# Output-projection products inside the attention's tail, a bank for the w1 sums, and w1 turns behind an exponential

## The chip, the cores and the metric

The kernel runs on one NeuronCore of a Trainium2 chip. The metric is the device time of one execution in microseconds (us); lower is better. A NeuronCore has TensorE (PE; its weight loads are shown as PEld), VectorE (DVE), ScalarE (ACT), GpSimd (POOL) and SyncE (SP), each with its own instruction queue that is worked in order, and 16 DMA engines. Here SP issues all loads. Accumulators lie in PSUM banks of 128 partitions by 512 floats.

## The reference

Two layers, each a single-token attention over a cache of 16384 positions and an MLP, both with residuals. The same weights and caches serve both layers. The kernel returns the output and the gradients of nine inputs.

```python
B, Sq, D = 2, 1, 1024
Hq, Hkv, Sk, Dh = 32, 4, 16384, 128      # F = 3584

def _A_ref(x, k_cache, v_cache, wq, wo):
    q = (x @ wq) -> [B, Hq, Sq, Dh]
    k, v = k_cache, v_cache repeated 8 times over heads
    p = softmax(einsum("bhqd,bhkd->bhqk", q, k) * Dh ** -0.5)
    return einsum("bhqk,bhkd->bhqd", p, v) reshaped to [B, Sq, Hq * Dh] @ wo

def _B_ref(x, w1, b1, w2, b2):
    return gelu(layernorm(x) @ w1 + b1) @ w2 + b2

x = x + _A_ref(layernorm(x), ...);  x = x + _B_ref(layernorm(x), ...)
x = x + _A_ref(layernorm(x), ...);  x = x + _B_ref(layernorm(x), ...)
# reference: this output, and its vjp for A_x, the caches, wq, wo, w1, b1, w2, b2
```

## The kernel before, in words

The program issues instructions in the order in which it is written; nothing reorders them between engines but semaphores. It runs the forward of layer 0, the forward of layer 1, the backward of layer 1, then the backward of layer 0 with the outputs.

*Loads.* Weights and cache tiles are 1 MB each and share one pool, `ld`, of `NLD` = 7 buffers. `w_take` (L353) takes the next buffer in turn and issues the load on SP's queue. A load waits there until the buffer's earlier contents have been read for the last time, and the loads behind it wait with it.

*A matrix times two columns.* `w_fwd` (L366) clears a part of the bank `ACCT` (called `acc_all` in the profile), then takes the tiles of a matrix one by one; `fwd_rows` (L358, its matmuls at L362) issues 32 matmuls for each, the weight tile as stationary operand, summing into the bank. wo has eight tiles, each of four heads of both batch rows; w1 has seven.

*Attention forward.* `attn_fwd` (L612) goes over eight groups `g` (batch row b = g // 4, key head g % 4), each of 16 slots. In a slot a piece of K is transposed (`emit_T`, L531), copied, and multiplied with the queries (`score`, L684). When a group's scores are complete, `post` plans its rest into later slots: maximum, 16 exponentials (`ex`, L648), 8 quads of 8 matmuls taken from a queue (`quad`, L563), each summing V times the exponentials into one half of `ACCT`: even groups the first half, odd groups the second. Then `evac` copies the sum out, `reduce` (L578) adds its parts, and `finish` (L661) scales the result into `oT`. The loop goes on after the 128 slots until the queue is empty: this is the tail, in which the groups 6 and 7 are finished. Afterwards two copies (L868) bring `oT` into `o_all`, the layout that wo's matmuls read, and wo is multiplied with `w_fwd`.

*MLP of layer 1.* `ln2_fwd` (L230) normalizes; w1 is multiplied through `w_fwd` with `keep`, an object `Back` that keeps the seven w1 tiles in their buffers for the backward and turns (transposes) them there: tiles 0 to 3 on VectorE (L294), tiles 4 to 6 on TensorE with copies by ScalarE (L395, L159). Two quarters of the tiles 4 and 5 are turned between the forward's tiles; what is left of 4 and 5 and one quarter of 6 come after the last one, ahead of the bias, the gelu (`g_u`, exponential at L894) and its slope. `weights_down` then multiplies the kept w1 tiles with the MLP's gradient `dh_all` (spread by `spg` and `Gw`, sums in the banks `dm_d` and `dm_p`, cleared in `banks`, L444 and L447), which frees their buffers for the backward's eight wo tiles; the backward attention follows.

PSUM banks of the kind `px` are handed out in turn, four of them.

Of the kernel before, what the change touches and what calls it, by code (L numbers as in the profile page):

```python
# [10 lines left out]
F32 = mybir.dt.float32  # L11
I32 = mybir.dt.int32
ACT = mybir.ActivationFunctionType
ALU = mybir.AluOpType
# [9 lines left out]
def kernel(  # L24
# [25 lines left out]
    V = nc.vector  # L50
# [3 lines left out]
    B, _, D = A_x.shape  # L54
    _, HKV, SK, DH = A_k_cache.shape
# [41 lines left out]
    def px(shape, dtype, name):  # L97
        return ps_x.tile(shape, dtype, name=name, tag="x")
# [46 lines left out]
    def copies_on(e):  # L145
        only["e"] = e
        load["A"] = load["D"] = 0.0
# [215 lines left out]
                          rhs=x[:, j0 + j, :].unsqueeze(1).to_broadcast([128, nw // 2, 2]),  # L363
                          start=False, stop=True, skip_group_check=True)

    def w_fwd(W, n_in, n_out, x, between=None, keep=None):  # L366
        JO = n_out // 128
        nw = min(WIDE, 512 // JO)
        fps = ACCT[:, 0:JO * nw].rearrange("p (j b) -> p j b", b=nw)
        V.memset(fps, 0.0)  # L370
        if keep is not None:
            keep.fps, keep.x, keep.nw = fps, x, nw
            for k in range(len(keep.tiles)):
                keep.load(k)
            last = len(keep.tiles) - 1
            for k in range(len(keep.tiles)):
                keep.forward(k)
                if keep.by_tile[k]:
                    keep.some(k)
                elif k < last:  # L380
                    keep.some(k, 2)
            return fps[:, :, 0:2]
        for j0, nj, c0, cw in w_tiles(W, n_in, n_out):
            fwd_rows(fps, nw, w_take(W, j0, nj, c0, cw), x, j0, c0 // 128)
            if between:
                between.popleft()()
        while between:
            between.popleft()()
        return fps[:, :, 0:2]
# [219 lines left out]
                sc_.later(2, a.reduce)  # L609
            sc_.q.append(fin)  # L610

    def attn_fwd(l, q_bf, rbc, oT, groups):  # L612
        sch = Sched()
        slots = [(g, c, b) for g in groups for c in range(NCH) for b in range(NB)]
        kTs, sc, st = {}, {}, {}

        def max_half(g, f):
            m = small.tile([128, 8], F32, name="mx%d" % f)
            V.tensor_reduce(out=m[:], in_=sc[g][f][:], axis=AX.X, op=ALU.max)
            charge("D", 0.7)  # L620
            st[g].append(m)

        def post(g):
            max_half(g, 1)
            m0, m1 = st[g]
            V.tensor_tensor(out=m0[:], in0=m0[:], in1=m1[:], op=ALU.max)
            esum = small.tile([128, 2, 8], F32, name="esum")
            negm = small.tile([128, 8], F32, name="negm")
            box = {}

            def p1():
                box["pm"] = pm_([8, 128], F32, "pm")
                PE.transpose(box["pm"][:, :], m0[:], identf[:])
                gm = small.tile([8, 1], F32, name="gm")
                V.reduce_max(out=gm[:], in_=box["pm"][:, :], axis=AX.X)
                box["dg"] = small.tile([8, 8], F32, name="dg")
                V.tensor_scalar(out=box["dg"][:], in0=identf[0:8, 0:8], scalar1=gm[:, 0:1], scalar2=None, op0=ALU.mult)
                charge("D", 0.5)

            def p2():  # L640
                pm2 = pm_([128, 8], F32, "pm2")
                PE.matmul(pm2[:], lhsT=onesf[0:8, :], rhs=box["dg"][:], start=True, stop=True)
                V.tensor_scalar(out=negm[:], in0=pm2[:], scalar1=-1.0, scalar2=None, op0=ALU.mult)  # L643
                charge("D", 0.2)

            def ex(f, h):
                half = NP // 2
                S.activation(out=e_all[:, g, f * half:(f + 1) * half, l, h, :],  # L648
                             in_=sc[g][f][:, h, :].rearrange("p (a b) -> p a b", b=2),
                             func=ACT.Exp, bias=negm[:, h:h + 1], scale=1.0, accum_out=esum[:, f, h:h + 1])  # L650
                charge("A", 0.3)

            def fin1():
                V.tensor_tensor(out=esum[:, 0, :], in0=esum[:, 0, :], in1=esum[:, 1, :], op=ALU.add)

            def fin2():
                pm3 = part_sum(esum[:, 0, :], 8, "pm3")
                V.reciprocal(out=rbc[:, g, :], in_=pm3[:])

            def finish(ps):  # L660
                V.tensor_tensor(out=oT[:, g, :], in0=ps, in1=rbc[:, g, :], op=ALU.mult)  # L661

            a = Acc(g, "V", lambda u: e_all[:, g, u, l].rearrange("p h t -> p (h t)"), finish, g % 2)
            sch.later(2, p1)
            sch.later(4, p2)
            for i in range(16):
                sch.later(5 + i // 2, lambda i=i: ex(i // 8, i % 8))
            sch.later(9, lambda: queue_acc(sch, a, range(0, 2), False))
            sch.later(13, lambda: queue_acc(sch, a, range(2, 4), True))
            sch.later(14, fin1)  # L670
            sch.later(15, fin2)

        def score(s):
            g, c, b = slots[s]
            if c == 0 and b == 0:
                sc[g] = {}
                st[g] = []
            kT = kTs.pop(s)
            for j in range(8):
                t = c * TC + b * 8 + j  # L680
                f = t // TH
                if t % TH == 0:
                    sc[g][f] = px([128, 8, TH], F32, "sc")
                PE.matmul(sc[g][f][:, :, t % TH], lhsT=kT[:, j, :], rhs=q_bf[:, g, :], start=True, stop=True)  # L684
            if c == NCH // 2 - 1 and b == NB - 1:
                max_half(g, 0)
            if c == NCH - 1 and b == NB - 1:
                post(g)

        cv = None  # L690
        s = 0
        while s < len(slots) + 2 or sch.busy():
            sch.s = s
            if s < len(slots):
                g, c, b = slots[s]
                if b == 0:
                    cv = kv_load("K", g, c)
                kTs[s] = emit_T(cv, b, True)
            sch.run_slot(1 if s < len(slots) else 2)
            if 2 <= s < len(slots) + 2:  # L700
                score(s - 2)
            s += 1

    def attn_bwd(l, do_bf, dqT, dn, groups, ahead):
# [148 lines left out]
    def lsl(l):  # L853
        return slice(2 * l, 2 * l + 2)

    def attn_layer_fwd(l, xT, between=None):
        y, rstd = ln_fwd(xT[:], f"a{l}")
        V.tensor_copy(out=n_all[:, 0:DJ, lsl(l)], in_=y[:])
        qps = w_fwd(A_wq, D, HD, n_all[:, 0:DJ, lsl(l)], between)
        qT_bf = vec.tile([128, G, 8], BF16, name=f"qT_bf{l}")  # L860
        for b in range(2):
            V.tensor_scalar(out=qT_bf[:, b * HKV:(b + 1) * HKV, :].rearrange("p k r -> p (k r)"), in0=qps[:, :, b],
                            scalar1=QSCALE, scalar2=None, op0=ALU.mult)
        rbc = vec.tile([128, G, 8], F32, name=f"rbc{l}")
        oT = vec.tile([128, G, 8], F32, name=f"oT{l}")
        attn_fwd(l, qT_bf, rbc, oT, ALLG)
        for b in range(2):
            V.tensor_copy(out=o_all[:, 0:HQ, 2 * l + b], in_=oT[:, b * HKV:(b + 1) * HKV, :].rearrange("p k r -> p (k r)"))  # L868
        aps = w_fwd(A_wo, HD, D, o_all[:, 0:HQ, lsl(l)])
        xn = vec.tile([128, DJ, 2], F32, name=f"xA{l}")  # L870
        V.tensor_tensor(out=xn[:], in0=aps, in1=xT[:], op=ALU.add)
        saved[f"a{l}"] = dict(y=y, rstd=rstd, qT_bf=qT_bf, rbc=rbc, oT=oT)
        return xn

    def mlp_hidden(l, xT, keep=None):
        y2, rstd2 = ln2_fwd(xT[:], f"m{l}")
        V.tensor_copy(out=m_all[:, 0:DJ, lsl(l)], in_=y2[:])
        if keep is not None:
            copies_on("A")
        hps = w_fwd(B_w1, D, F, m_all[:, 0:DJ, lsl(l)], keep=keep)  # L880
        if keep is not None:
            for k in range(len(keep.tiles)):
                keep.some(k, 1 if k == len(keep.tiles) - 1 else 4)
            copies_on(None)
        hpre = vec.tile([128, FJ, 2], F32, name=f"hpre{l}")
        V.tensor_tensor(out=hpre[:], in0=hps, in1=b1T[:].to_broadcast([128, FJ, 2]), op=ALU.add)
        x2 = wrk.tile([128, FJ, 2], F32, name="g_x2")
# [5 lines left out]
        z = wrk.tile([128, FJ, 2], F32, name="g_z")  # L893
        S.activation(out=z[:], in_=u[:], func=ACT.Exp, scale=2.0 * GELU_C)  # L894
        if keep is not None:
            V.tensor_scalar(out=x2[:], in0=x2[:], scalar1=3.0 * GELU_A * GELU_C * 0.5, scalar2=GELU_C * 0.5,
                            op0=ALU.mult, op1=ALU.add)
            V.tensor_tensor(out=x2[:], in0=x2[:], in1=hpre[:], op=ALU.mult)
# [55 lines left out]
    def weights_down(l, gT, name, mid=None):  # L954
        sv = saved[f"m{l}"]
        w1b = sv.pop("w1", None)
        if w1b is None:
            w1b = w1_back()
            for k in range(len(w1b.tiles)):
                w1b.load(k)  # L960
        w1b.banks()
        w1b.open(dh_all[:, 0:FJ, lsl(l)])
        copies_on("A")
        if l == 1:
# [738 lines left out]
```

## Time and profile before

| | |
|---|---|
| times of three runs | 1116.38, 1118.36, 1119.42 us; median 1118.36 |
| the profiled execution | 1124.0 us, of which 1122.2 us from the first to the last instruction (span) |
| busy: PE, PEld, DVE, ACT, POOL | 919.0, 674.1, 615.2, 532.3, 69.0 us |
| DMA | 441.83 MB, mean 394 GB/s over the span |
| granted TensorE clock, mean | 0.852 of full |
| forward attention of layer 1, its last result | at 419.06 us |
| w1 forward of layer 1, first and last matmul | 432.79 to 446.7 us |
| first product with a kept w1 tile | at 453.79 us |

Busy time is time in which an engine had an instruction in work. The chain of work that ended last is followed back from the last instruction, at each step to what released it. A line of the timeline gives start, duration, engine, source line, operation, output and inputs, and in brackets the idle time before it with what ended it. For DMA issues, start and duration are those of the issue on SP's queue, not of the transfer. All times are counted from the start of the span.

### The profile page before, as it was taken

The numbers are of one execution on the slowest core, as the hardware profiler recorded it, in microseconds if no ns is written. First come the engines' busy times: TensorE is split into PE (matmuls) and PEld (weight loads), VectorE is DVE, ScalarE is ACT, GpSimd is POOL, SyncE is SP. The second block draws the span as 40 slices with busy tenths as digits, with TensorE's granted clock in tenths as the row PEclk, the third lists the DMA queues.
The fourth block names the chain that finished last, engine by engine and source line by source line (L and its number), as shares of the span: only waits on it lengthen the run. The fifth ranks groups of instructions, "written<-read, shape, count | busy, mean of one in ns | idle before, by whom it ended". The sixth has DMA issues, their size and how long they took to land.

```text
span 1122.2 us, 37948 instructions
## 1 busy us (share of the span) xinstructions
PE 919.0 (82%) x16706; PEld 674.1 (60%) x16707; DVE 615.2 (55%) x1333; ACT 532.3 (47%) x1352; POOL 69.0 (6%) x122
## 2 busy tenths in 40 slices
PE   3979796458889886789987877889898896999996
PEld 3867674357677656678765676655554453455552
DVE  1545442071355434554443357479698775787776
ACT  0535352004545341334433234468587775686765
POOL 0000000000000000000000000022021111111210
PEclk9989786557899876899988899999799897797878
DMA  9999999999999988799999999998999999999997
GB/s 370 423 424 425 423 425 415 395 413 420 423 413 424 423 311 302 287 426 420 387 415 422 392 398 327 376 355 312 405 367 420 424 418 424 405 400 420 422 408 290
DMA packets 99973, 441.83 MB, mean 394 GB/s; under 512 B 7126, under 2 KB 10198, under 8 KB 62688
## 3 DMA queue, kind: packets, MB, share of 16 engines
q1 hardware_dynamic: 82464, 347.12, 76.7%
q0 software_dynamic: 17344, 92.29, 20.0%
q8 instruction: 130, 2.13, 0.7%
q14 instruction: 35, 0.29, 0.1%
HBM read 340.80 MB, written 98.58 MB: 392 GB/s over the span
## 4 chain that ended last, share of the span: by engine, by line
PE 50%; DMA 31%; DVE 11%; ACT 4%; issue 4%; POOL 0%; DVEq 0%; SPq 0%; POOLq 0%; ACTq 0%
DMA kv_V<-in_A_v_cache_dram 10%; PE tp L531 10%; DMA wt<-in_B_w_dram 5%; PE tpm L1610 5%; DMA kv_K<-in_A_k_cache_dram 5%; PE acc_all L563 4%; PE xm L1419 4%; DMA wt<-in_A_wo_dram 4%; PE xm L1333 3%; PE sc L684 3%; PE dp L1472 3%; PE wtp L395 2%; DMA keepK<-in_A_v_cache_dram 2%; PE dp L779 2%; DMA out_dram<-keepK 2%
## 5 line engine op out<-in xcount | busy, mean ns | idle before, releaser
L159 ACT COPY kT<-tp 128x512 int32<-128x512 int32 x201 | 118.0, 587 | 289.3 <-PE tp L531 277.0
L162 DVE COPY kT<-tp 128x1024 bf16<-128x1024 bf16 x167 | 114.2, 691 | 136.5 <-PE tp L531 126.3
L531 PE MATMUL tp<-ident,kv_K 128*128 128x128 bf16 x1728 | 145.3, 233 | 4.0 <-DMA kv_K<-in_A_k_cache_dram 3.7
L531 PEld LDWEIGHTS <-kv_K 128*128 128x128 bf16 x1728 | 110.2, 104 | 4.8 <-DMA kv_K<-in_A_k_cache_dram 4.5
L170 DVE CAST big<-xm 128x512 bf16<-128x512 f32 x133 | 86.4, 685 | 23.7 <-PE xm L1419 13.4
L167 ACT CAST big<-xm 128x512 bf16<-128x512 f32 x151 | 82.1, 595 | 24.9 <-PE xm L1333 13.4
L684 PEld LDWEIGHTS <-kT 128*128 128x128 bf16 x2048 | 76.3, 98 | 27.6 <-issue 22.1
L684 PE MATMUL sc<-qT_bf,kT 128*128 128x8 bf16 x2048 | 91.8, 171 | 0.0
L167 ACT CAST keepV<-xm 128x512 bf16<-128x512 f32 (+1 forms) x137 | 75.1, 594 | 32.2 <-PE xm L1419 20.3
L362 PEld LDWEIGHTS <-wt 128*128 128x128 bf16 x1920 | 57.2, 104 | 54.6 <-DMA wt<-in_B_w_dram 16.6
L159 ACT COPY wt<-wtp 128x512 int32<-128x512 int32 x70 | 39.0, 587 | 89.9 <-PE wtp L395 79.4
L648 ACT ACTIVATE e_all<-sc,negm 128x64 bf16<-128x64 f32 x256 | 77.2, 342 | 1.1 <-DVE negm L643 1.0
L170 DVE CAST keepV<-xm 128x512 bf16<-128x512 f32 (+1 forms) x101 | 66.0, 685 | 21.1 <-PE xm L1419 14.2
L531 PE MATMUL tp<-ident,kv_V 128*128 128x128 bf16 x864 | 70.1, 228 | 5.8 <-DMA kv_V<-in_A_v_cache_dram 4.4
L563 PE MATMUL acc_all<-kv_V,e_all 128*16 128x256 bf16 x864 | 46.6, 296 | 28.9 <-DMA kv_V<-in_A_v_cache_dram 13.8
L294 DVE STREAM_TRANSPOSE wt<-wt 128x512 int32<-128x512 int32 x106 | 64.5, 674 | 7.7 <-PE w2b_f L362 5.6
L531 PEld LDWEIGHTS <-kv_V 128*128 128x128 bf16 x864 | 55.5, 102 | 7.6 <-DMA kv_V<-in_A_v_cache_dram 4.7
L648 ACT ACTIVATION_READ_ACCUMULATOR e_all<-sc,negm 128x1 f32 x256 | 59.4, 232 | 0.0
L167 ACT CAST keepK<-xm 128x512 bf16<-128x512 f32 x98 | 52.8, 595 | 11.5 <-PE xm L1419 7.5
L1472 PE MATMUL dp<-wdo,kT 128*128 128x64 bf16 x896 | 52.7, 206 | 0.0
L1419 PE MATMUL xm<-QmK,blk 64*128 64x512 bf16 x256 | 47.7, 437 | 2.3 <-ACT keepV L167 1.0
L170 DVE CAST keepK<-xm 128x512 bf16<-128x512 f32 x69 | 44.8, 684 | 8.6 <-PE xm L1419 6.6
(380 smaller groups left out, 1557.7 us busy)
## 6 DMA issues: line engine op xcount, KB each, us to landing
kv_K<-in_A_k_cache_dram SPq DMA_DIRECT2D x81, 1024.0 KB, 12.5
kv_V<-in_A_v_cache_dram SPq DMA_DIRECT2D x81, 1024.0 KB, 12.0
wt<-in_B_w_dram SPq DMA_DIRECT2D x35, 1024.0 KB, 12.9
wt<-in_A_wo_dram SPq DMA_DIRECT2D x32, 1024.0 KB, 8.7
out_dram<-big POOLq DMA_DIRECT2D x26, 1024.0 KB, 17.1
out_dram<-keepV POOLq DMA_DIRECT2D x19, 1024.0 KB, 17.5
out_dram<-keepK POOLq DMA_DIRECT2D x17, 1024.0 KB, 16.2
wt<-in_A_wq_dram SPq DMA_DIRECT2D x16, 1024.0 KB, 10.9
```

Of the source, the lines that this page charges most:

```text
L159: S.copy(out=dst.bitcast(I32), in_=src.bitcast(I32))
L162: V.tensor_copy(out=dst, in_=src)
L167: S.copy(out=dst, in_=src)
L170: V.tensor_copy(out=dst, in_=src)
L294: V.transpose(out=w, in_=w)
L362: PE.matmul(fps[:, o0 + o, :].rearrange("p (a b) -> p a b", b=2), lhsT=wv[:, j, o * 128:(o + 1) * 128], rhs=x[:, j0 + j, :].unsqueeze(1).t ...
L531: PE.transpose(tp[:, j, :], cv[:, b * 8 + j, :], ident[:])
L563: PE.matmul(self.acc[cg:cg + 16, :], lhsT=coef(u), rhs=self.cv[:, t:t + 2, :].rearrange("p t d -> p (t d)"), start=False, stop=True, tile_ ...
L648: S.activation(out=e_all[:, g, f * half:(f + 1) * half, l, h, :], in_=sc[g][f][:, h, :].rearrange("p (a b) -> p a b", b=2), func=ACT.Exp, ...
L684: PE.matmul(sc[g][f][:, :, t % TH], lhsT=kT[:, j, :], rhs=q_bf[:, g, :], start=True, stop=True)
L1419: PE.matmul(pss[k][:], lhsT=blk[p:p + 64, o + 2 * h + k // 2, :], rhs=Qm[p:p + 64, :, :].rearrange("p a b -> p (a b)"), start=True, stop=T ...
L1472: PE.matmul(dp[:, :, t:t + 4], lhsT=kT[:, j, :], rhs=wd[:, :, x:x + 4], start=(b + j == 0), stop=False)
```

## The change

The change concerns four places of the forward.

1. `finish` writes each group's result twice, first into `o_all`, then into `oT`; the two copies after the attention go.
2. `attn_fwd` calls `tail(step)` after each slot beyond the 128th, where the step counts from 0. In layer 1, at step 6, `tail` clears the first half of `ACCT`, issues the first seven loads of wo, multiplies tile 0, issues the load of tile 7 and multiplies tile 1; at the steps 7 to 10 it multiplies the tiles 2 to 5. Tiles 0 to 5 hold the heads of the groups 0 to 2 and 4 to 6; tiles 6 and 7 need groups 3 and 7 and follow the attention. In layer 0 all eight tiles follow the attention as before. In TensorE's order, tiles 0 to 4 now stand ahead of the first quad of group 7, tile 5 behind it, then the other 40 matmuls of the first part, the row sums and the last 16. The order of SP's loads stays as it was.
3. At step 9 a `px` bank `h_ps` is taken and cleared, and layer 1's w1 sums go there and not into `ACCT`; the clearing between the layernorm and w1 goes. The clearing of `dm_d` and `dm_p` moves from behind `dh_all` into the layernorm, behind its first row sum.
4. The rest of TensorE's w1 turns is issued behind the exponential of the gelu: in ScalarE's order the exponential stands ahead of five copies that it stood behind. TensorE's own order is the same there.

```diff
-    def w_fwd(W, n_in, n_out, x, between=None, keep=None):
+    def w_fwd(W, n_in, n_out, x, between=None, keep=None, bank=None):
         JO = n_out // 128
         nw = min(WIDE, 512 // JO)
-        fps = ACCT[:, 0:JO * nw].rearrange("p (j b) -> p j b", b=nw)
-        V.memset(fps, 0.0)
+        fps = (ACCT if bank is None else bank)[:, 0:JO * nw].rearrange("p (j b) -> p j b", b=nw)
+        if bank is None:
+            V.memset(fps, 0.0)
...
-    def attn_fwd(l, q_bf, rbc, oT, groups):
+    def attn_fwd(l, q_bf, rbc, oT, groups, tail=lambda step: None):
...
             def finish(ps):
+                kv = g % HKV
+                V.tensor_tensor(out=o_all[:, kv * 8:(kv + 1) * 8, 2 * l + g // HKV], in0=ps, in1=rbc[:, g, :], op=ALU.mult)
                 V.tensor_tensor(out=oT[:, g, :], in0=ps, in1=rbc[:, g, :], op=ALU.mult)
...
+            if s >= len(slots):
+                tail(s - len(slots))
             s += 1
...
-        attn_fwd(l, qT_bf, rbc, oT, ALLG)
-        for b in range(2):
-            V.tensor_copy(out=o_all[:, 0:HQ, 2 * l + b], in_=oT[:, b * HKV:(b + 1) * HKV, :].rearrange("p k r -> p (k r)"))
-        aps = w_fwd(A_wo, HD, D, o_all[:, 0:HQ, lsl(l)])
+        tiles = w_tiles(A_wo, HD, D)
+        fps = ACCT[:, 0:DJ * WIDE].rearrange("p (j b) -> p j b", b=WIDE)
+        wvs = {}
+
+        def take(k):
+            wvs[k] = w_take(A_wo, *tiles[k])
+
+        def prod(k):
+            fwd_rows(fps, WIDE, wvs.pop(k), o_all[:, 0:HQ, lsl(l)], tiles[k][0], 0)
+
+        def tail(step):
+            if l == 0:
+                return
+            if step == 6:
+                assert 0 not in Acc.in_use
+                V.memset(fps, 0.0)
+                for k in range(NLD):
+                    take(k)
+                prod(0)
+                take(NLD)
+            if 6 <= step < 11:
+                prod(step - 5)
+            if step == 9:
+                h_bank[l] = px([128, 512], F32, "h_ps")
+                V.memset(h_bank[l][:, 0:FJ * (512 // FJ)], 0.0)
+
+        attn_fwd(l, qT_bf, rbc, oT, ALLG, tail)
+        if l == 0:
+            V.memset(fps, 0.0)
+            for k in range(len(tiles)):
+                take(k)
+                prod(k)
+        else:
+            for k in list(wvs):
+                prod(k)
+        aps = fps[:, :, 0:2]
...
     def mlp_hidden(l, xT, keep=None):
-        y2, rstd2 = ln2_fwd(xT[:], f"m{l}")
+        y2, rstd2 = ln2_fwd(xT[:], f"m{l}", keep.banks if keep is not None else lambda: None)
...
-        hps = w_fwd(B_w1, D, F, m_all[:, 0:DJ, lsl(l)], keep=keep)
-        if keep is not None:
-            for k in range(len(keep.tiles)):
-                keep.some(k, 1 if k == len(keep.tiles) - 1 else 4)
-            copies_on(None)
+        hps = w_fwd(B_w1, D, F, m_all[:, 0:DJ, lsl(l)], keep=keep, bank=h_bank.get(l))
...
         S.activation(out=z[:], in_=u[:], func=ACT.Exp, scale=2.0 * GELU_C)
         if keep is not None:
+            for k in range(len(keep.tiles)):
+                keep.some(k, 1 if k == len(keep.tiles) - 1 else 4)
+            copies_on(None)
             V.tensor_scalar(out=x2[:], in0=x2[:], scalar1=3.0 * GELU_A * GELU_C * 0.5, scalar2=GELU_C * 0.5,
                             op0=ALU.mult, op1=ALU.add)
...
             w1b = w1_back()
             for k in range(len(w1b.tiles)):
                 w1b.load(k)
-        w1b.banks()
+            w1b.banks()
         w1b.open(dh_all[:, 0:FJ, lsl(l)])
```

More of the change, by code (lines that the diff above doesn't have):

```diff
@@ L854, in lsl @@
         return slice(2 * l, 2 * l + 2)
+    h_bank = {}
     def attn_layer_fwd(l, xT, between=None):
```

## The prediction

> **What bounds the kernel now.** I read the page first: over the span the DMA engines are near full (394 GB/s) and TensorE is busy 82%, so the useful place to look is where DMA is *not* full. The chain of work that ended last, between 410 and 460 us (start, length, what):
>
> ```profile
> 410.05 4.86 ACT e_all L648 x32
> ...
> 419.85 6.18 PE acc_all L362 x224
> ...
> 426.39 14.06 DMA wt<-in_B_w_dram
> 440.50 1.02 PE acc_all L362 x32
> ...
> 449.77 0.59 ACT wt L159
> 450.35 0.16 ACT g_z L894
> ```
>
> Seven wo tiles are multiplied only after the attention has ended (224 matmuls from 419.85), then the chain waits for w1 tiles, then the gelu's exponential sits behind ScalarE's copies of turned w1 tiles. Next, busy time by stretches of 4 us (span, PE, PEld, DVE, ACT, POOL, PEclk, DMA share, GB/s):
>
> ```profile
> 412.00:416.00 4.00, 2.94 (x49) 1.47 (x49) 0.17 (x1) 2.90 (x20) 0.00 (x0) 0.50 0.98 377
> 416.00:420.00 4.00, 2.65 (x28) 1.92 (x29) 1.31 (x6) 0.00 (x0) 0.00 (x0) 0.50 0.10 37
> 420.00:424.00 4.00, 4.00 (x156) 4.00 (x154) 0.00 (x0) 0.00 (x0) 0.00 (x0) 0.50 0.44 108
> 424.00:428.00 4.00, 2.74 (x104) 2.64 (x101) 0.00 (x0) 0.00 (x0) 0.00 (x0) 0.81 1.04 401
> ...
> 444.00:448.00 4.00, 3.77 (x70) 3.47 (x68) 1.12 (x6) 1.97 (x4) 0.00 (x0) 0.75 0.08 26
> 448.00:452.00 4.00, 1.54 (x24) 1.33 (x22) 1.37 (x7) 2.09 (x5) 0.00 (x0) 1.00 0.00 0
> 452.00:456.00 4.00, 2.26 (x96) 2.07 (x95) 1.82 (x9) 0.00 (x0) 0.00 (x0) 0.60 0.02 4
> ```
>
> DMA stands still twice: about 6 us (0.90x4 + 0.56x4 = 5.8) around 420, and 12.5 us from 444.3 to 456.8. Why the first: the waits of SP's queue, and the instruction that its wait holds (us in total, times, longest; then start, duration):
>
> ```profile
> SPq L356 <- PE acc_all L362: 17.4, 6, 11.3
> ```
>
> ```profile
> 409.18 0.37 SPq L356 DMA_DIRECT2D wt<-in_A_wo_dram  x1
> 420.89 0.37 SPq L356 DMA_DIRECT2D wt<-in_A_wo_dram  x1
> ```
>
> Tile 6 of wo is issued at 409.18, tile 7 only at 420.89: all seven load buffers are full of wo tiles, and the first is freed when its 32 matmuls are done. The eighth tile of wo and seven of w1 stand behind that one wait.
>
> **The change, part by part, against the profiled span of 1122.2 us.** *The loads of wo tile 7 and w1.* Group 6's result is written at 410.80 (`oT`, 0.17). In the new order the result row, the copy to `oT`, and the memset of the sums (0.27) follow on a VectorE that is idle until 414.93; TensorE starts wo tile 0 at about 411.5. A tile is 32 matmuls at 27.6 ns (6.18 us / 224) = 0.88 us. SP's order is unchanged, so tile 7 is issued near 412.4, w1 tiles 0 to 3 near 413.3 to 416, and tile 4 after wo tile 5 near 417.4. Tile 6's load takes 8.8 us from issue to landing (median of that one issue), so it lands at 418.0. A landing follows the last by 2.6 us in a fed queue (w1 matmuls that wait for DMA start at 435.32, 437.94, 440.50), so tile 7 lands at 420.6; before, its matmuls started at 427.27. Shift 6.7 us. The w1 tile that decides is the fifth: before, it started 13.23 us after wo tile 7 (440.50), and from there TensorE runs without a gap (two rounds of 16 turns at 1.72 between three tiles) to 446.7. Bounds of the shift at that tile: 7.2 if every tile takes 2.55 us after 418.0; 5.7 if the handover is as in layer 0, where the queue was never empty and the fifth w1 tile came 14.24 us after wo's last (205.79 to 220.03). I take **6.7**, the spacing of this very stage.
>
> *Does anything else become last?* TensorE: tiles 0 to 4 (4.4 us) end at 415.9, quads of group 7 8x64 ns, tile 5 0.88, 40 quads at 59 ns (1.88/32) 2.4, row sums and 16 quads 1.5 (415.95 to 417.5 before), evacuation 0.44, `o_ps` 1.02, result 0.17: attention ends at 422.8, 3.4 us later than before (419.4). But only 64 matmuls remain (1.8 us), so `xA` comes at 424.7 instead of 428.27. Layernorm to `m_all` takes 3.9 us (428.27 to 432.16); the two `dm` memsets (0.27 each) fill the 0.49 us wait for its row sum; the memset of 504 columns (0.48) moves from behind `m_all` to VectorE's idle time near 412, into a bank of its own. w1 starts at 428.7, tiles 0 to 3 (four of 1.02) end at 432.8, the fifth lands at 433.8: one us of slack. VectorE turns w1 tiles 0 to 3 (16 in 9.61 us), from 429.1 to 438.7; `hpre` is due at 440.0: 1.3 us of slack. So 3.6 us of earlier `xA` are hidden by the stream; without it they would be the gain. wo tiles 4 and 5 must be in place at 415.0 and 416.4; counting back from 418.0 by 2.6 they land at 412.8 and 415.4. Group 7's 48 quads stand behind them on TensorE.
>
> *The exponential.* `g_u` ends at 447.69, the exponential ran at 450.25, behind five copies of 0.53 to 0.59. In front of them it runs at 447.72, and its result is used at 448.0 instead of 450.53: 2.5 us. What it displaces: the last three rounds of TensorE's turns need banks that those copies free. From the first copy (now 448.0) to the end of the fifth round it took 2.52 us (447.21 to 449.73), so TensorE is free at 450.5, and `dh_all` is ready at 450.3: nearly level. `spg` 0.29, then `Gw` 0.40 without two memsets ahead of it (it began at 453.33, after 452.87 + 0.54): first `dm_d` product at 451.3 against 453.79, 2.5 us. That is with the granted clock of 1.00 of the row at 448. At 0.50 eight turns take 0.87 instead of 0.46 (the forward's `tp` pieces), the fifth round ends 0.7 us later: 1.75. Gain 1.75 to 2.5, I take **2.2**, since the shifted stage begins near an edge of a clock stretch.
>
> On that clock the Trainium skill ("TensorE: Matmul & The Clock Gate", Part 4: PE-mode transpose) says that transposes do not count as busy for the clock gate. The row at 448, granted 1.00 after 4 us made up mostly of turns, doesn't bear that out; by the rule the term would be 1.75.
>
> *Small parts.* Eight more result writes of 0.17 in each layer lie under VectorE's idle time; in layer 0 the two copies (0.32) and the wait for them go, but its loads run without a pause (DMA share 1.01 to 1.05 from 160 to 245), so nothing is gained; without that cover it would be 0.2.
>
> *Behind it.* The first `dm_d` product frees the first buffer for the backward's wo loads (issued 454.86 before), and from 456.8 to 640 DMA share is 1.00: a fed stream, whose end moves with its start. Sum 6.7 + 2.2 = **8.9**: span 1122.2 to 1113.3. The profiled execution took 1124.0; the median of three is 1118.36 (1116.38 to 1119.42), so 1118.4 - 8.9 = **1109.5**.
>
> A rule speaks against the first term: the Trainium skill ("DMA: Bandwidth & Descriptors", Specifications) puts HBM at about 358 GB/s a core. The rows of this stage show 401, and 377 where it ran out. By the rule a tile of 1.05 MB takes 2.9 us, and eight behind 418.0 would gain some 2.3 us less.
>
> **Rivals.** *A: as summed*, own range 7.5 to 9.7 (5.7 + 1.75, 7.2 + 2.5) and a us or so of spread either way: 1107 to 1112.
>
> *B: another wait takes the place.* VectorE's turns or TensorE's order become last. If w1 starts 2 us later than reckoned, its turns end at 440.7 and `hpre` loses 0.7; if the turns behind the exponential also hold `spg` for all of what it saved, 2.2 go. For it: slacks of only 1.0 and 1.3 us. Against: both are computed at the lower clock, and 3.4 us stretches of steady matmuls should raise it (the row at 424 shows 0.81 after the busy one at 420). 1118.4 - 6.0 = 1112.4.
>
> *C: it doesn't do what it says.* Tile 7's load is not issued earlier, or its gain is hidden. Were SP held until the attention's end, the first term is gone and the second stays under the spread: 1116. For it: SP's queue is one line, and everything waits behind one release. Against: the release is tile 0's last matmul, in the new order ahead of group 7's quads.
>
> *D: slower.* The backward and the stores, 490 to 1122, run at granted clocks of 0.92, 0.91 and 0.87, and stretches of it move with the phase of the work. Price: 0.41 us per eight turns at half clock. To eat 8.9 and lose another 3.4, 30 groups of eight must fall to half clock, some 40 us of the 632 at a group per 1.3 us. For it: TensorE holds half of the chain. Against: the three runs before, whose phases differ too, lie within 3.0 us. About 1122.
>
> **How the numbers follow.** A 0.68, B 0.14, C 0.11, D 0.07. About 0.3% (3.4 us, 1115.0) can be told from no change. A and B are faster (0.82, and 0.03 of C and D), C is mostly no change, D mostly slower: 0.85, 0.09, 0.06. The time is A's, 1109.5. For 8 in 10 the range takes A and B whole and a part of C: 1105.5 to 1114.5; its lower end leaves room for TensorE at full clock in the attention's tail, which A's sum doesn't count.
>
> **What would show it.** Right: tile 7 of wo issued near 412.4; no row with a DMA share under 0.9 between 412 and 436; `xA` near 424; the fifth w1 tile's matmuls near 433.8; the exponential within 0.1 us of `g_u`; the first `dm_d` product near 444.9; the backward's first wo issue 8.9 us earlier. Wrong: a pause of DMA near 420 that remains, w1 matmuls that no longer wait for DMA, a TensorE wait for ScalarE just before `spg` over 1 us, or the 8.9 us there at 480 and not at the end.

## The result, and the profile after

| | before | changed | ratio, 95% interval |
|---|---|---|---|
| first comparison, 4 runs each | 1118.89 us (1116.38 to 1119.85) | 1108.88 us (1107.22 to 1109.43) | 0.9904 [0.9875, 0.9933] |
| second comparison, 17 and 6 runs | 1118.20 us (1113.78 to 1123.47) | 1108.37 us (1103.49 to 1110.11) | 0.9908 [0.9886, 0.9929] |

The change takes off 10.0 us in the first comparison and 9.8 in the second. The profiled execution of the changed kernel took 1108.78 us with a span of 1107.0. The one of before had 1122.2, which is 15.2 more; that difference must not be read as the change, as is shown below.

The chain of waits after (start, length, what), for the stretch whose chain of before stands in the prediction:

```profile
410.44 3.98 PE acc_all L362 x143
414.42 1.90 issue
416.32 0.64 PE acc_all L362 x17
...
424.03 1.86 PE acc_all L362 x64
...
430.26 3.56 PE h_ps L362 x128
433.83 1.02 PE h_ps L362 x32
...
437.09 0.31 issue
...
441.14 0.23 DVE g_u L927
441.39 0.25 ACT g_z L929
441.64 0.48 ACT wt L159
```

Of the 224 wo matmuls that stood in one piece behind the attention, 64 are left (424.03). The link of 14.06 us in which the chain waited for w1's transfers is gone: 160 w1 matmuls follow each other from 430.26, and from 408 to 446 us the chain has no DMA link at all, in both profiles of the changed kernel. What ends last in this stretch is now TensorE's order through the attention's tail, no longer the stream of loads. The exponential stands directly behind `g_u`, and the first copy behind it. New are long links called "issue", of which this stretch of the chain before had none over 0.05 us: 1.90 us in which TensorE waited for nothing that the profile names, in the middle of a wo tile, and 0.31 us among the w1 tiles.

Busy time by stretches of 4 us after (span, PE, PEld, DVE, ACT, POOL, PEclk, DMA share, GB/s):

```profile
412.00:416.00 4.00, 2.42 (x91) 2.31 (x87) 0.17 (x1) 1.91 (x14) 0.00 (x0) 0.50 1.05 405
416.00:420.00 4.00, 3.68 (x89) 2.69 (x93) 0.00 (x0) 0.00 (x0) 0.00 (x0) 0.50 1.06 411
420.00:424.00 4.00, 3.21 (x38) 2.01 (x27) 0.85 (x4) 0.00 (x0) 0.00 (x0) 0.50 1.04 401
...
432.00:436.00 4.00, 4.00 (x114) 3.90 (x111) 4.00 (x7) 0.25 (x1) 0.00 (x0) 0.50 0.99 368
436.00:440.00 4.00, 3.69 (x77) 3.54 (x75) 4.00 (x8) 1.88 (x4) 0.00 (x0) 0.57 0.38 131
440.00:444.00 4.00, 2.93 (x55) 2.58 (x53) 3.43 (x16) 2.49 (x6) 0.00 (x0) 1.00 0.00 0
444.00:448.00 4.00, 2.48 (x157) 2.14 (x157) 0.97 (x3) 0.58 (x1) 0.00 (x0) 1.00 0.27 88
448.00:452.00 4.00, 3.57 (x104) 3.38 (x103) 0.45 (x1) 1.66 (x3) 0.00 (x0) 1.00 0.99 326
```

The pause of DMA around 420 (share 0.10 and 0.44 before) is filled: 1.04 to 1.06. The second pause remains and lies earlier, from about 438 to 447. Read down the DMA column: what the change removes is idle transfer time, and the second hole, 9 us of it, is what is left in this region. The cause of the first pause, on SP's queue, is gone too (start, duration of the issues):

```profile
411.49 0.37 SPq L356 DMA_DIRECT2D wt<-in_A_wo_dram  x1
412.35 8.93 SPq L356 DMA_DIRECT2D wt<-in_B_w_dram  x5
```

wo tile 7 is issued 1.6 us after group 6's result (409.91), and the w1 loads follow at once.

How far the gain travels (times from the start of each span; the kernel before and the changed one were each profiled twice):

| event | before | before, 2nd | changed | changed, 2nd |
|---|---|---|---|---|
| wo tile 6 lands | 417.95 | 418.25 | 418.22 | 417.79 |
| wo tile 7 lands | 427.22 | 427.89 | 420.78 | 420.35 |
| fifth w1 tile lands | 440.45 | 440.84 | 433.78 | 433.32 |
| layer 1's attention sums `xA` | 428.27 | 428.94 | 425.91 | 426.04 |
| hidden sums `hpre` | 446.74 | 447.13 | 440.41 | 440.57 |
| first `dm_d` product | 453.79 | 454.17 | 444.82 | 444.98 |
| first wo load of the backward | 454.86 | 455.24 | 445.50 | 445.65 |
| backward attention begins | 488.37 | 490.81 | 479.30 | 479.88 |
| its layer-0 sums begin (`xM`) | 669.82 | 670.30 | 660.46 | 660.80 |
| from there to the end | 452.4 | 443.7 | 446.5 | 445.8 |

Up to the `xM` row, pair against pair, the change is worth 9.4 to 9.5 us (at single marks on the way 9.0 to 10.9); the medians of the runs say 9.8 to 10.0. The last row is a stretch with the same code in all four, and it varies by 8.7 us between two executions of the same kernel. So the ends of two traces can't be compared for a change of this size; a stage in front of that stretch can.

### The profile page after: what moved, and what is told of

Same layout as the page of the kernel before. It is cut to its first block, busy times and chain, and to the rows that moved or that the text cites. A ratio compares the mean times of both kernels' runs of the same rounds, so it can differ in the third digit from the quotient of the medians.

```text
span 1107.0 us, 37959 instructions
## 1 busy us (share of the span) xinstructions
PE 904.7 (82%) x16706; PEld 667.4 (60%) x16707; DVE 615.9 (56%) x1345; ACT 531.0 (48%) x1352; POOL 68.7 (6%) x122
## 4 chain that ended last, share of the span: by engine, by line
PE 51%; DMA 29%; DVE 12%; issue 4%; ACT 3%; POOL 0%; SPq 0%; DVEq 0%; ACTq 0%; POOLq 0%
PE tp L532 11%; DMA kv_V<-in_A_v_cache_dram 9%; PE acc_all L564 5%; PE tpm L1648 5%; DMA kv_K<-in_A_k_cache_dram 5%; DMA wt<-in_B_w_dram 4%; PE xm L1457 4%; DMA wt<-in_A_wo_dram 4%; PE sc L687 3%; PE xm L1371 3%; PE dp L1510 3%; PE wtp L396 2%; DMA keepK<-in_A_v_cache_dram 2%; PE dp L784 2%; DMA out_dram<-keepK 2%
## 5 line engine op out<-in xcount | busy, mean ns | idle before, releaser
L687 PEld LDWEIGHTS <-kT 128*128 128x128 bf16 x2048 | 76.3, 98 | 27.6 <-issue 22.1
L564 PE MATMUL acc_all<-kv_V,e_all 128*16 128x256 bf16 x864 | 46.4, 295 | 27.6 <-DMA kv_V<-in_A_v_cache_dram 13.3
L1457 PE MATMUL xm<-QmV,blk 64*128 64x512 bf16 x240 | 42.4, 397 | 10.6 <-ACT keepK L167 5.5
```

The costliest lines, as they stand in the source:

```text
L564: PE.matmul(self.acc[cg:cg + 16, :], lhsT=coef(u), rhs=self.cv[:, t:t + 2, :].rearrange("p t d -> p (t d)"), start=False, stop=True, tile_ ...
L1457: PE.matmul(pss[k][:], lhsT=blk[p:p + 64, o + 2 * h + k // 2, :], rhs=Qm[p:p + 64, :, :].rearrange("p a b -> p (a b)"), start=True, stop=T ...
```

## The experiments

*One part alone, and all but one part.* Three kernels and the same runs of before (1116.88 us, 1113.06 to 1125.09, 23 runs).

`tail_only`: the parts 1 and 2 of the change, without the bank of its own and with the turns ahead of the gelu.

```diff
             if 6 <= step < 11:
                 prod(step - 5)
-            if step == 9:
-                h_bank[l] = px([128, 512], F32, "h_ps")
...
-        y2, rstd2 = ln2_fwd(xT[:], f"m{l}", keep.banks if keep is not None else lambda: None)
+        y2, rstd2 = ln2_fwd(xT[:], f"m{l}")
```

> The wo products in the tail and the result rows alone; w1 sums, their clearing, the clearing of dm_d and dm_p, and the exponential as before. Stream theory (the earlier loads of wo tile 7 and w1 are the larger term): DMA does not pause between 412 and 436, the fifth w1 tile's matmuls start within 0.5 us of where the full change has them counted from group 6's result, and the time is 5 to 6.5 us under before. Rival (the clearing of banks off the path is a large part): at most 4 us under before.

Measured 1111.81 us, ratio 0.9943 [0.9918, 0.9969]: 5.1 us. In its trace the fifth w1 tile lands at 433.02 and `hpre` comes at 439.33, which is 15.41 and 21.72 us after wo tile 6's landing (417.61). In the two profiles of the full change it is 15.56 and 15.53, 22.19 and 22.78: the clearings of banks, which the full change has in addition, bring nothing that shows here.

`exp_only`: the kernel before, with the rest of the turns behind the exponential.

```diff
-        if keep is not None:
-            for k in range(len(keep.tiles)):
-                keep.some(k, 1 if k == len(keep.tiles) - 1 else 4)
-            copies_on(None)
         hpre = vec.tile([128, FJ, 2], F32, name=f"hpre{l}")
...
         S.activation(out=z[:], in_=u[:], func=ACT.Exp, scale=2.0 * GELU_C)
         if keep is not None:
+            for k in range(len(keep.tiles)):
+                keep.some(k, 1 if k == len(keep.tiles) - 1 else 4)
+            copies_on(None)
```

> The old kernel with only the rest of TensorE's w1 turns behind the gelu's exponential. Theory (terms add): from hpre to the first dm_d product 4.6 to 5.2 us in place of 7.05 (the two clearings still ahead of Gw), the first backward wo issue 2 to 2.5 us earlier, time 1.7 to 2.7 us under before. Rival (the turns behind the exponential hold spg as long as they did ahead of it): under 1 us.

Measured 1116.12 us, ratio 0.9991 [0.9973, 1.0009]. The runs alone can't tell 2 us from nothing. The trace can: from `hpre` to the first `dm_d` product it takes 4.50 us (447.18 to 451.68, a tenth under the forecast) against 7.05 and 7.04 in the two profiles of before, and the first wo issue of the backward comes at 452.36, 2.5 and 2.9 us earlier.

`no_exp`: the full change with the turns left ahead of the gelu (the same edit, backwards).

> The full change without the exponential's move. Theory (terms add): 2 to 2.7 us slower than the full change, that is 7 to 8 us under before; against the tail alone up to 1 us better through the clearings. Rival (the move gives nothing once the stream is early): the time of the full change.

Measured 1112.07 us, ratio 0.9952 [0.9932, 0.9972]: some 5 us under before, where 7 to 8 were forecast; the interval (3.1 to 7.6 us) still takes in the lower part of the forecast. ScalarE's queue in its profile (start, duration, line, what; idle before, releaser in brackets) shows what the exponential stands behind:

```profile
441.13 0.58 ACT L159 COPY wt<-wtp 128x512 int32<-128x512 int32 x1 [1.12 <-PE wtp L396]
441.98 0.58 ACT L159 COPY wt<-wtp 128x512 int32<-128x512 int32 x1 [0.27 <-PE wtp L396]
442.75 1.09 ACT L159 COPY wt<-wtp 128x512 int32<-128x512 int32 x2 [0.19 <-PE wtp L396]
444.03 0.58 ACT L159 COPY wt<-wtp 128x512 int32<-128x512 int32 x1 [0.19 <-PE wtp L396]
444.51 0.25 ACT L933 ACTIVATE g_z<-g_u 128x56 f32<-128x56 f32 x1
```

`hpre` was there at 440.26, and the exponential runs 4.25 us later, behind five copies; in the full change it runs 0.98 us after `hpre`. From `hpre` to `dm_d` this kernel takes 7.70 us; the granted clock was 0.69 and 0.74 in its rows of 440 and 444, where the kernel before had 0.75 and 1.00 in those of 444 and 448, so a part of the 7.70 may be slower turns.

*The sum of the parts.* `full_again`: the full change in the second comparison.

> The full change once more, beside the parts on the same chip. If the tail (5.1 us measured alone) and the move of the turns (2.2 forecast, 2.55 in the trace of the part that has it alone) add up, it is 7.0 to 8.5 us faster than before, ratio 0.9925 to 0.9938; if the two need each other, more than 8.5.

Its ratio is that of the table, 0.9908 [0.9886, 0.9929]; the median, 9.8 us, lies above the band for adding, but the interval (7.9 to 12.7 us) takes the band's upper end in. The runs of the parts alone sum to less, 5.1 + 0.8 = 5.9 us, but each of these figures has an interval of 2 to 3 us on either side. The traces are sharper. At the first `dm_d` product `tail_only` (446.36) is 7.43 and 7.81 us ahead of the two profiles of before, `exp_only` (451.68) 2.11 and 2.49, together 9.5 and 10.3; the full change is 8.8 to 9.4 ahead. In the traces the two parts add within about a microsecond, and nothing of the gain needs both.

*Is it the stream, or the work taken off TensorE's path?* Two things come earlier in the full change: the w1 transfers (the fifth tile by 6.7 and 7.5 us) and `xA` (by 2.4 and 2.9). The first kernel meant to part them, `late_free`, multiplied the tiles in another order, to free the first buffer later.

```diff
-                prod(0)
-                take(NLD)
...
-                prod(step - 5)
+                for k in {6: (1, 2), 7: (3,), 8: (4,), 9: (0,), 10: (5,)}[step]:
+                    prod(k)
+            if step == 9:
+                take(NLD)
```

> The full change with the five products ahead of group 7's quads in the order 1, 2, 3, 4, 0 and tile 7's load behind them: the same work for TensorE in the same places, but wo's first buffer is freed about 5 us later. Stream theory: tile 7 issued near 416.5 in place of 411.5, a pause of DMA of about 2 us near 418, tile 7 landing 6.3 us after its issue (422.8 for 420.8), the fifth w1 tile and everything behind 2 to 2.5 us later than in the full change; time 7 to 8.5 us under before. Rival (it is the earlier sum xA, TensorE's order, that sets the gain): the time of the full change, within 0.5 us by the trace.

Measured 1109.67 us, ratio 0.9939 [0.9921, 0.9958]. This says nothing on the question, because the load didn't come late: it was issued at 412.99, 1.6 us after group 6's result (411.41) as in the full change, when the first product in the new order, tile 1's, had freed its buffer. In its place `hold_w1` holds SP's queue behind wo tile 7 until the attention is nearly over.

```diff
+            if step == 16:
+                hold = vec.tile([128, 16], BF16, name="hold")
+                V.memset(hold[:], 0.0)
+                nc.sync.dma_start(hold[:], B_w1[0:128, 0:16])
```

> The full change, with one small load (the first 16 columns of w1, into a tile that nothing reads) put in SP's queue behind the load of wo tile 7; VectorE clears that tile after the last group's reciprocal, so SP waits there until about 421.5, and the loads of w1 are issued as late as before, while wo tile 7 and all of TensorE's moved work stay early. Stream theory: the fifth w1 tile lands at 437.9 to 438.6 instead of 433.78, the hidden sums and everything behind come 4.1 to 4.8 us later than in the full change, time 1113 to 1114 beside 1108.9 (4 to 5 us behind the full change's own run here), while xA stays at 425.9 within 0.5. Rival (what gains is TensorE's work that was moved off the path, xA 2.4 us earlier): time within 1 us of the full change.

Measured 1115.29 us, ratio 0.9969 [0.9953, 0.9985]: it gives back about 0.6 of the 0.9 per cent. SP's issues, the stretches, and TensorE's w1 matmuls in its profile:

```profile
421.08 0.34 SPq L898 DMA_DIRECT2D hold<-in_B_w_dram  x1
421.52 11.03 SPq L356 DMA_DIRECT2D wt<-in_B_w_dram  x7
```

```profile
416.00:420.00 4.00, 3.82 (x97) 2.77 (x97) 0.00 (x0) 0.00 (x0) 0.00 (x0) 0.65 0.51 198
420.00:424.00 4.00, 3.21 (x81) 2.59 (x74) 0.89 (x5) 0.00 (x0) 0.00 (x0) 0.92 0.33 48
```

```profile
433.19 1.02 PE L362 MATMUL h_ps<-m_all,wt 128*128 128x18 bf16 x32 [1.47 <-DMA wt<-in_B_w_dram]
435.75 1.02 PE L362 MATMUL h_ps<-m_all,wt 128*128 128x18 bf16 x32 [1.54 <-DMA wt<-in_B_w_dram]
438.29 1.02 PE L362 MATMUL h_ps<-m_all,wt 128*128 128x18 bf16 x32 [1.51 <-DMA wt<-in_B_w_dram]
```

Idle DMA of 4.6 us is back (0.49x4 + 0.67x4), each w1 tile is waited for again, the fifth lands at 438.24 and `hpre` comes at 444.61. Yet `xA`, at 424.56, is even earlier than in the full change. From wo tile 6's landing (417.53) to `hpre` it takes 27.08 us, against 22.19 and 22.78 in the full change and 28.79 and 28.88 before. The 1.7 us that stay of the gain fit wo tile 7, which still comes early: one tile less, of some 2.6 us, stands ahead of w1. So while w1's loads come late, the earlier `xA` is worth nothing that shows. The opposite isn't shown: no run has the loads early and `xA` as late as before. In the full change TensorE reaches the w1 tiles only after they have landed, and from `xA` to `hpre` it takes 14.50 and 14.53 us; with `xA` at 428.27, as before, `hpre` would come at about 442.8 (an estimate from these rows) in place of 440.4, so some 2.4 us of the gain need the moved work too. The runs lost some 6.8 us where 4 to 5 were expected; the trace shows 4.3 to 4.9 up to `hpre` and 4.0 to 4.4 at the first `dm_d` product (449.02) and at `xM` (664.86). The two intervals together leave about 3 us of room on either side, so the difference isn't telling.

*What is the stall inside the wo products?* `spread` puts group 7's score-value matmuls between them.

```diff
                 prod(0)
                 take(NLD)
-            if 6 <= step < 11:
-                prod(step - 5)
+                prod(1)
+            for k in {13: (2, 3), 14: (4, 5)}.get(step, ()):
+                prod(k)
```

> The full change, with products 2 to 5 behind the last score-value matmuls of group 7, two at a time, so that TensorE doesn't run 143 pairs of wo in one go. Theory of the instruction blocks: the 1.90 us stall inside wo's products shrinks to between 0 and 1.2, and what is left of it lies at the same count of TensorE instructions (pair 7273 of the trace); xA comes 0.5 to 1.5 us earlier than 425.91. Stream theory of the gain: the fifth w1 tile still lands at 433.8 within 0.3, hidden sums and time unchanged (within 0.5 us at the hidden sums). Rival (TensorE's order is what ends last at the hidden sums): they come earlier by as much as xA, up to 1.5 us. Rival for the stall (it waits for data of wo tile 4): it stays 1.9 us and sits at the first matmul of a tile.

Measured 1109.22 us, ratio 0.9924 [0.9902, 0.9946], not to be told from the full change. TensorE in its profile:

```profile
411.18 1.87 PE L362 MATMUL acc_all<-o_all,wt 128*128 128x32 bf16 x64 [0.65 <-DVE acc_all L888]
412.97 1.88 PE L564 MATMUL acc_all<-keepV,e_all 128*16 128x256 bf16 x32
414.79 1.37 PE L362 MATMUL acc_all<-o_all,wt 128*128 128x32 bf16 x47
417.18 0.59 PE L362 MATMUL acc_all<-o_all,wt 128*128 128x32 bf16 x17 [1.02 <-issue]
```

The stall is 1.02 us instead of 1.90 and 2.07 in the two profiles of the full change. It follows 64 + 32 + 47 = 143 matmuls, of other kinds than the 143 before, and sits in the middle of tile 3 and not of tile 4: it goes with the count and not with the data. (The expectation names pair 7273; that is the next such place. The stall is behind TensorE's 6888th weight load in both traces.) The forecast that `xA` comes 0.5 to 1.5 us earlier isn't borne out: it comes 14.98 us after group 6's result, but in the two profiles of the full change that is 16.00 and 14.87, and in absolute time it is 0.29 and 0.42 earlier. The two profiles of the full change differ by 1.1 us with nearly the same stall, and the granted clock differs: in the row of 420 it was 0.50 in the first and 0.78 in the second, and there the last 16 score-value matmuls and `o_ps` took 1.03 and 1.02 us in the first, 0.61 and 0.61 in the second. `hpre` (440.00) moved with `xA`, by 0.4 and 0.6 against the two profiles of the full change, while the fifth w1 tile landed at 433.39, within the 433.32 and 433.78 of those two: here the rival has a point. TensorE's last w1 tile (438.97 + 0.99) and VectorE's last turn (439.98) end level, just ahead of `hpre`.

`pad64` shifts the count and leaves the code: 64 extra pairs of weight load and matmul at the start of layer 1, into a bank that nothing reads.

```diff
     def attn_layer_fwd(l, xT, between=None):
+        if l == 1:
+            pad = pm_([128, 8], F32, "pm")
+            for i in range(64):
+                PE.matmul(pad[:], lhsT=ident[:], rhs=ident[:, 0:8], start=True, stop=True)
```

> The full change with 64 pairs of weight load and matmul (identity by identity, into a bank that nothing reads) added on TensorE at the start of layer 1, where it waits for the layernorm: every later instruction of TensorE moves 128 places on in its queue. Theory of the instruction blocks (256 instructions, which are 128 pairs, are fetched at a time): the stall inside wo's products comes after 79 matmuls instead of 143, and as the block before was asked for earlier it is shorter, 0.3 to 1.5 us instead of 1.9 to 2.1; it ends again 2.2 to 2.6 us after the start of a 16 KB packet of the instruction queue; the stall among the w1 tiles (about 437.4) and that at 452.85 to 454.68 move or go as well. Rival (the stall belongs to this place of the code, to its data or its clock): it stays after 143 matmuls with 1.9 to 2.1 us. Time: within 3 us of the full change, as nothing but the stalls moves.

One run, 1109.27 us, beside 1117.30 for the kernel before. TensorE in its profile:

```profile
409.97 4.41 PE L362 MATMUL acc_all<-o_all,wt 128*128 128x32 bf16 x160 [0.65 <-DVE acc_all L892]
...
417.23 1.82 PE L564 MATMUL acc_all<-keepV,e_all 128*16 128x256 bf16 x33 [0.93 <-issue]
...
434.43 0.90 PE L362 MATMUL h_ps<-m_all,wt 128*128 128x18 bf16 x28 [1.17 <-issue]
```

All 160 wo matmuls run without a stall. The expected rest after 79 of them isn't there; the 16 KB packet that fits this place began at 407.18, long before TensorE got there (about 412.1). The next stall comes 128 weight loads later, in the middle of eight score-value matmuls, and that of the w1 tiles has moved from 437.09 to 433.26 and grown from 0.31 to 1.17 us; the one at 452.85 is gone, as forecast. The stall belongs to the count of instructions, which is shown; the rival, data or clock at that place, falls. In this run `xA` comes at 424.27, TensorE is through four w1 tiles at 432.18 and waits 0.81 us for the fifth: with `xA` that early the stream is last again.

*The stretch behind.* `before_again`: the kernel before, for a second profile.

> The kernel before, for a second profile of it: the stretch from the backward's layer-0 sums (xM, 669.82 in the profile shown) to the end took 451.9 us there, and 443 to 448 in the five kernels with the same code behind it. Theory that this is spread of that stage and no effect of the change: 443 to 450 here. If the change itself shortens that stage: about 452 again.

One run, 1115.72 us; from `xM` to the end 443.2 us by the same marks as the 451.9 of the expectation (both counted from a mark 0.5 us behind the `xM` row of the table). So nothing shows that the change shortens that stage; the first profile of before was a long sample of it.

## Why the prediction was right, step by step

*The stream term, 6.7.* Right in its mechanism and nearly in size. wo tile 7 was issued 1.6 us after group 6's result, as reckoned; tile 6 landed at 418.22 (418.0 foretold), tile 7 at 420.78 (420.6), the fifth w1 tile's matmuls began at 433.83 (433.8). Against the landing of wo tile 6, which hardly moves, the fifth w1 tile's landing gained 7.0 us (22.50 and 22.59 became 15.56 and 15.53) and `hpre` 6.0 to 6.7 (28.79 and 28.88 became 22.19 and 22.78). `hold_w1` shows by taking the early w1 loads away that the earlier `xA` doesn't bring this by itself.

*The slacks behind it.* This is the step that was mis-sized. The prediction had TensorE one microsecond ahead of the stream at the fifth w1 tile, and `xA` 13.9 us after group 6's result (424.7 against 410.80), 3.6 us earlier than before. It came 16.00 and 14.87 us after that result, 2.4 and 2.9 us earlier. The sum had no term for the stalls of 1.90 and 2.07 us inside wo's products; how much of them reaches `xA` differs with the clock that was granted behind them (see `spread`), so their exact share isn't shown. From `xA` to the first w1 matmul it took 4.35 us, where 4.0 were reckoned. The slack was gone: in the first profile TensorE reached the fifth tile at 433.83, and the tile had landed at 433.78. A second stall of 0.31 and 0.46 us among the w1 tiles came on top. VectorE's last turn ended at 440.27, TensorE's last w1 matmul at 440.37, and `hpre` began at 440.41. Three chains end within a few tenths, so rival B did set in, though not with the 2.9 us that it was priced at: `hpre` came 6.63 and 7.25 us after the fifth tile's landing in the two profiles of the full change, where 6.29 was enough in both of before. That is the 0.3 to 1.0 us by which the 7.0 at the landing shrank on the way to `hpre`. The prediction had itself named "w1 matmuls that no longer wait for DMA" as a sign of being wrong. The sign appeared; it cost little only because the chain that took over ended so close behind the stream.

Slacks of a microsecond are also smaller than what moves from one execution to the next. Group 6's result came 7.15 and 6.79 us before wo tile 6 landed in the two profiles of before, and 8.31 and 6.62 us in those of the changed kernel.

*The exponential term, 2.2.* Too small: 7.05 and 7.04 us from `hpre` to `dm_d` became 4.41 in both profiles, 2.6 less. The prediction chose between 2.5 at full clock and 1.75 at half. In the first profile the stretch was granted 1.00 from 440 to 452, so the upper end was right; in the second the row of 440 was granted 0.72, and the term was the same. VectorE and TensorE at that place after the change:

```profile
443.74 0.22 DVE L984 TENSOR_TENSOR dh_all<-gb_d,dh_up 128x56 bf16<-128x56 f32 x1
```

```profile
443.44 0.61 PE L396 MATMUL wtp<-ident,wt 128*128 128x128 bf16 x8 [0.19 <-ACT wt L159]
444.01 0.27 PE L303 MATMUL spg<-dh_all,ident 128*32 128x16 bf16 x16
444.82 1.09 PE L321 MATMUL dm_d<-wt,Gw 128*8 128x128 bf16 x64 [0.55 <-DVE Gw L306]
```

The last turns end at 444.05 and `dh_all` is ready at 443.96: level, as reckoned, so the turns cost nothing behind the exponential. The clock rule on transposes that the prediction weighed (the Trainium skill, "TensorE: Matmul & The Clock Gate", Part 4: PE-mode transpose) again finds no support: of TensorE's work from 440.4 to 444.05 every matmul was a turn, and the rows of 440 and 444 were granted 1.00. Other matmuls had kept TensorE busy before 440, so this doesn't decide how turns count.

*Small parts.* In layer 0 nothing moved, as reckoned: the first result of layer 1's attention came at 308.79 and 308.81 us before and at 309.07 and 308.66 after. The bank of its own shows no gain that could be told: `no_exp`, which has it, and `tail_only`, which hasn't, are 1112.07 and 1111.81.

*Behind it.* The gain of 9.0 to 9.2 at `dm_d` is 9.4 to 9.6 at the first wo load of the backward and 9.4 to 9.5 at `xM`, 215 us later: as reckoned, a fed stream whose end moves with its start. Rival C falls by the issue at 411.49, D by the runs. The rule on HBM's rate, by which the term would have lost 2.3 us, did not bind here: the filled stretch has rows of 401 to 411 GB/s. (The 2.3 us count eight tiles behind 418.0; the fifth w1 tile is the sixth, so it would have been six times 0.33, 2.0 us.)

The sum of 8.9 comes so near to the measured 9.8 to 10.0, and to the 9.4 to 9.5 of the traces, partly by luck: a first term 0 to 0.7 too large and a second 0.4 too small met, and the chain that replaced the stream ended only tenths of a microsecond behind it.

## What to carry to other kernels

Look for the stretch in which the DMA engines stand idle, and then for the one instruction on which the head of the load queue waits; moving that single release ahead can be worth what all the loads behind it gain, while moving work off a compute engine's path may be worth nothing as long as the loads come late, as `hold_w1` shows. When such a hole is filled, the chains beside it end nearly level, so each slack of a microsecond has to be reckoned with every stall that the new order can bring. Measure an effect of a few microseconds at a mark close behind it and against a mark that the change can't move, since a later stage with the same code may swing by more.

## What the runs showed of the hardware

TensorE can run out of instructions. The profile has a DMA queue of the kind "instruction" (the changed kernel's page, section on queues: packets, MB, share of 16 engines):

```profile
q8 instruction: 130, 2.13, 0.7%
```

That is 16 KB a packet, and 130 packets are one for every 257 of TensorE's 33413 instructions (16706 matmuls and 16707 weight loads on the same page). In the stretch read here, the "issue" stalls of TensorE lie behind counts of weight loads that differ by 128 or a multiple of it, but for a single instruction between: 6888, 7273, 7529 and 7657 in the changed kernel, and 7016 and 7273 in `pad64`. Each ends 2.2 to 2.6 us after such a packet began: 414.01 and 416.31, 435.14 and 437.40, 445.89 and 448.21, 452.10 and 454.68 in the first profile of the changed kernel. It is not a matter of this stretch alone. Over the whole span of that profile TensorE has 17 "issue" stalls of more than 0.25 us, 14.9 us in all (12 with 11.7 us in the first profile of before), and every one ends 2.2 to 2.6 us after such a packet began.

In this stretch the packet itself begins 2.9 to 4.2 us after TensorE passed the place 128 pairs earlier where DMA is full, and 0.8 to 1.2 us after it where DMA stands still (near 437 to 445). If that passing is what asks for the block, a block takes 5.2 to 6.5 us from asking to use with full DMA, while 128 wo matmuls take 3.5 (27.6 ns each, a row of before). Where TensorE has slower work in between, as for most of the 130 blocks, no such stall is seen.

The Trainium skill ("Runtime: NRT & Kernel Launch", Instruction fetch mechanics) says that the instructions come in blocks of 16 KiB, 256 instructions, over a queue of their own, and that crossing a boundary is mostly hidden. The size and the queue agree with the traces (a pair is two instructions). Hidden it was not where small matmuls ran without a break under full DMA: 1.02 to 2.07 us for a block among the wo products of the kernels here that have them in one or two pieces, and 1.83 us in the backward at 452.85. The second profile of the kernel before has one of 0.87 us too, behind the 7016th weight load, among its 224 wo matmuls.
